# Keeping fourteen units of V and two heads' output weights on the chip between two attention layers

## The chip, the cores and the metric

The kernel runs on one core of one Trainium2 chip. The metric is the time of one execution in microseconds on the device. Before the change three runs took 177.41 to 177.56 us, with a median of 177.49 us.

## The reference, cut to what matters

Four tokens pass through attention, a gated layer, the same attention and the same gated layer again. Both attentions use the same weights and the same caches, and both gated layers the same three matrices, so everything that is read for the first half is needed again for the second half.

```
x = x + A(layernorm(x), k_cache, v_cache, wq, wo)
x = x + B(layernorm(x), w_gate, w_up, w_down)
x = x + A(layernorm(x), k_cache, v_cache, wq, wo)
x = x + B(layernorm(x), w_gate, w_up, w_down)

A: q = x @ wq               4 tokens, D = 512, 32 query heads of 128
   k, v = last 2048 rows of the caches, 8 heads shared by 4 query heads each
   softmax(q k / sqrt(128)) v, then @ wo
B: (sigmoid(x @ w_gate) * (x @ w_up)) @ w_down     inner size 1792
```

## The kernel before

**What is where.** Everything is counted in units of 256 columns of bf16 over 128 partitions, 64 KB. One head's K or V (four tokens' caches, 2048 rows each) is 32 units, 2 MB. `kt` holds the K of all eight heads (256 units) and stays for both attentions. `wo_sb` holds the output weights of all eight heads (64 units, 8 a head) and stays too. `arena` (75 units), `side` (31 units), `pb` and `pt` take turns with the rest. `pt` also holds the softmax weights of two heads at a time. `WHERE` (L426 to L442) says at which units each V and each weight matrix lies. V does not stay: attention 1 reads all of it into the arena, and attention 2 reads all of it again, the first two heads into `arena` and `side` and the other six into K blocks that attention 2 has done with.

**PSUM.** There are eight banks. In attention 1 banks 0 to 2 take the transposes of K (L728, copied out at L738), bank 3 the scores, 4 the turned softmax weights, 5 and 6 the products with V, and 7 sums the output projection. The first gated layer has its sums in banks 0, 1 and 2, and the second q projection (`project_q`, L678) in bank 5. In attention 2 banks 3 and 0 take the scores of even and odd heads, 1 and 2 the turned weights.

**The order of work.** `_Plan` records operations with the tokens they read and write. `_schedule` (L95) places them on the engines by estimated durations; `_assign_sync` (L185) gives each wait a semaphore. The DMAs alone stand in the order in which the program names them, all on SP's queue: SP waits until the destination of the next transfer is free, issues it (L456, in `dma`), and goes on. A transfer whose place is freed late holds back all behind it.

**Attention, head by head.** `scores` (L742) multiplies q with K (L751), takes the row maximum (L760 to L770), the exponential (ACT, L773), and turns the result (L779, L784). `weights` (L791) spreads it into `pt` (L806 on DVE, L813 on ACT). `pv_wo` (L863) multiplies with V, at L841 for heads marked in `WIDE` (followed by a copy at L849 and a sum at L856) and at L883 for the others, scales (L893), selects (L919, L926) and applies the output weights (L934). After head 6, `early_residual` (L941) takes the sum out of bank 7: a copy on ACT (L947), a subtraction on DVE (L953), eight matmuls on PE (L960) and an addition (L966). Head 7 goes a short way of its own (L904, L551, L554).

**Between the attentions** lies the first gated layer (`glu`, L1007): u01 and g01 (the first half of `w_up` and `w_gate`, which stay for the second gated layer), g23, u23, then `w_down` in pieces d0, d4, d8, d10, d12. g23 and d8 share arena units, so the transfer of d8 waits until the matmuls with g23 are over. Then the 32 units of `wq` that did not stay are read (q01), then V for attention 2.

**The end.** V of heads 6 and 7 arrives last, then g23, u23 and `w_down` for the second gated layer. Head 7's V comes in pieces of 16, 8 and 8 units.

```
WHERE["V0_%d" % (HKV - 1)] = [ar(0, 16), ar(16, 8), ar(24, 8)]
...
    "V2_0": [ar(22, 14), sx(0, 8), sx(8, 8), sx(16, 2)],
    "V2_1": [sx(18, NS - 18), ar(0, UHEAD - NS + 18)],
...
for h in range(2, HKV):
    WHERE["V2_%d" % h] = [("kt", (h - 2) * UHEAD + u, n)
                          for u, n in (((0, 16), (16, 8), (24, 8)) if h == HKV - 1 else ((0, UHEAD),))]
```

Of the kernel before, what the change touches and what calls it, by code (L numbers as in the profile page):

```python
# [6 lines left out]
BF16 = mybir.dt.bfloat16  # L7
ACTF = mybir.ActivationFunctionType
# [6 lines left out]
class _Op:  # L15
    __slots__ = ("idx", "eng", "name", "dur", "emit", "deps", "odeps", "users", "start", "finish",
                 "sem", "val", "inc", "dma_bytes", "dma_rate", "waits", "prio", "ndeps_left")

    def __init__(self, idx, eng, name, dur, emit):
        self.idx = idx  # L20
        self.eng = eng
        self.name = name
        self.dur = dur
        self.emit = emit
        self.deps = set()
        self.odeps = set()
        self.users = []
        self.start = 0.0
        self.finish = 0.0
        self.sem = None  # L30
        self.val = 0
        self.inc = 1
        self.dma_bytes = 0
        self.dma_rate = 0.0
        self.waits = ()
        self.prio = idx
        self.ndeps_left = 0
# [147 lines left out]
def _assign_sync(ops, order, n_dma_sems):  # L185
    counts = {}
    dma_i = 0
    for e in ENGINES:
        for o in order[e]:
            if o.sem is not None:  # L190
                sem = o.sem
            elif e == "sync":
                sem = ("dma", dma_i % n_dma_sems)
                dma_i += 1
                o.inc = 16
# [72 lines left out]
def build(nc, A_x, A_k, A_v, A_wq, A_wo, B_wg, B_wu, B_wd, out):  # L268
# [15 lines left out]
    NCH = 4  # L284
# [21 lines left out]
    WIDE = {0: {0: 4, 1: 4, 2: 4, 3: 4, 4: 4, 5: 4, 6: 2}, 2: {2: 2, 3: 2, 4: 2, 5: 2}}  # L306
    HEADS1 = list(range(HKV))
# [29 lines left out]
    with es:  # L337
# [24 lines left out]
        rz = sb("rz", [128, NPT * NR], F32)  # L362
# [40 lines left out]
        def blk_ap(s):  # L403
            return {"kt": kt, "ar": arena, "pt": pt, "pb": pb, "sx": side}[s[0]][:, s[1] * UNIT:(s[1] + s[2]) * UNIT]
# [15 lines left out]
        def ar(u, n):  # L420
            return ("ar", u, n)
# [5 lines left out]
        for h in range(HKV - 1):  # L427
            WHERE["V0_%d" % h] = [ar(MAIN - UHEAD if h % 2 == 0 else 0, UHEAD)]
        WHERE["V0_%d" % (HKV - 1)] = [ar(0, 16), ar(16, 8), ar(24, 8)]
        WHERE["u01"], WHERE["g01"] = ar(MAIN - 2 * GU, 2 * GU), ar(MAIN - 4 * GU, 2 * GU)  # L430
        WHERE.update({
            "g23_1": ar(32, 2 * GU), "u23_1": ar(0, 2 * GU),
            "d0_1": ar(14, 8), "d4_1": ar(22, 8), "d8_1": ar(32, 4), "d10_1": ("pb", 0, 4), "d12_1": ("pt", 4, 4),
            "q01": [ar(36, 10), ar(0, 14), ar(14, 8)],
            "V2_0": [ar(22, 14), sx(0, 8), sx(8, 8), sx(16, 2)],
            "V2_1": [sx(18, NS - 18), ar(0, UHEAD - NS + 18)],
            "g23_3": ar(22, 2 * GU), "u23_3": sx(0, 2 * GU),
            "d0_3": ar(0, 8), "d4_3": ar(8, 8), "d8_3": ar(38, 8), "d12_3": sx(14, 4),
        })
        for h in range(2, HKV):  # L440
            WHERE["V2_%d" % h] = [("kt", (h - 2) * UHEAD + u, n)
                                  for u, n in (((0, 16), (16, 8), (24, 8)) if h == HKV - 1 else ((0, UHEAD),))]  # L442
# [19 lines left out]

        def load_v(L, h):
# [3 lines left out]
            for s in WHERE["V%d_%d" % (L, h)]:  # L467
                n = s[2]
                dma("V%d_%d_%d" % (L, h, u0), blk_ap(s), v_d[h][:, :, u0 * UNIT:(u0 + n) * UNIT], w=blk_tok(s),
                    rate={32: "bw_16k", 16: "bw_8k"}.get(n, "bw_4k"), nbytes=128 * n * UNIT * 2)  # L470
# [207 lines left out]
        def project_q(L, pieces, pieces_last):  # L678
            if not L:
                return project_first(pieces, pieces_last)  # L680
            prev = []
            toks = []
            wid = NB
            for n, (ap, tk, ktc, q0, q1) in enumerate(pieces):
                def e_q(pe, ap=ap, ktc=ktc, q0=q0, q1=q1, st=(n == 0), last_ktc=pieces_last):
                    last = None
                    for q in range(q0, q1):
                        last = pe.matmul(ps[:, QB, q * wid:(q + 1) * wid],
                                         ap[:, (q - q0) * 128:(q - q0 + 1) * 128],
                                         xn[:, ktc * (NB + 1):ktc * (NB + 1) + wid],  # L690
                                         start=(st and q == q0), stop=(ktc == last_ktc),
                                         skip_group_check=True)
                    return last
                prev = [P.op("tensor", "qproj%d_%d" % (L, n), tm["pe_pair"] * (q1 - q0), e_q,
                             r=list(tk) + [("xn",)], w=[("psq", n)], banks=(QB,), order=prev)]
                toks.append(("psq", n))

            def scaled(src, r, banks):
                P.op("vector", "q_evac%d" % L, c_dve(HQ * NB),
                     lambda v: v.tensor_tensor(  # L700
                         qs[:, 28:28 + HKV * NB * STRIP].rearrange("p (h b s) -> p h b s", h=HKV, b=NB)[:, :, :, 0:REP],
                         src.rearrange("p (h r b) -> p h b r", h=HKV, r=REP)[:, :, 0:NB, :],
                         rstd[:, :].unsqueeze(1).unsqueeze(3).broadcast_to([128, HKV, NB, REP]),
                         ALU.mult),
                     r=r + [("rstd",)], w=[("qs",)], banks=banks)
            if True:
                mc = means(L, tq, cs_q, HQ)
                P.op("vector", "q_mean%d" % L, c_dve(HQ * NB),
                     lambda v: v.tensor_tensor(tq[:, :], ps[:, QB, 0:HQ * NB], tq[:, :], ALU.subtract),
                     r=toks + [mc], w=[mc], banks=(QB,))  # L710
                scaled(tq[:, :], [mc], ())
# [30 lines left out]
        def scores(L, n, h, sbk, tbk):  # L742
# [14 lines left out]
            P.op("tensor", "S%d_%d" % (L, h), 16 * tm["pe_s"] * (0.55 if L == 0 else 1.0), e_s, r=kr + [("qs",)], w=[("pss", sbk)], banks=(sbk,))  # L757
# [32 lines left out]

        def weights(L, n, h, tbk):  # L791

            k2 = n % 2
            kp = n % NPT
            ptv = pt[:, kp * NJ4 * NR:(kp + 1) * NJ4 * NR]
            pk = blk_tok(("pt", kp * NR // 4, NR // 4))
# [31 lines left out]
        def wide_pv(L, n, h, wide, bank, out, s):  # L828

            kp = n % NPT  # L830
# [4 lines left out]
            def e_pv(pe):  # L835
                last = None
                for i, (tv, q, c) in enumerate(steps):
                    w0 = (kp * NJ4 + (tv * NB + q) * NCH + c) * NR
# [3 lines left out]
                                     pt[:, w0:w0 + rows], v,  # L842
                                     start=(i < groups), stop=(i >= len(steps) - groups), skip_group_check=True)
                return last
            P.op("tensor", "PV%d_%d" % (L, h), 1800.0, e_pv,
                 r=blk_tok(s) + blk_tok(("pt", kp * NR // 4, NR // 4)) + (("pa", kp),), w=[("pvw", bank)], banks=(bank,))
# [16 lines left out]
        def pv_wo(L, n, h, pbk, pieces, prev=()):  # L863
            k2 = n % 2
            kp = n % NPT
            wide = WIDE[L].get(n, 0)
            obk = pbk[k2] if L else 6 if wide else 5
# [5 lines left out]
            for s, j0 in () if wide else pieces:  # L873
                def e_pv(pe, s=s, j0=j0):
                    last = None
                    for j in range(j0, j0 + s[2] * UNIT // 128):

                        q, c, tv = j // NJ, j % NJ // CB, j % CB
                        w0 = (kp * NJ4 + (tv * NB + q) * NCH + c) * NR
# [5 lines left out]
                                         pt[:, w0 - odd * NR:w0 + (2 - odd) * NR],  # L885
                                         start=(j == 0), stop=(j == NJ4 - 1), skip_group_check=True)
                    return last
                prev = [P.op("tensor", "PV%d_%d_%d" % (L, h, j0), s[2] * UNIT // 128 * tm["pe_pair"], e_pv,
                             r=blk_tok(s) + blk_tok(("pt", kp * NR // 4, NR // 4)) + (("pa", kp),), w=[("pso", obk, j0)], banks=(obk,), order=prev)]
# [79 lines left out]
        GB, UB, YB = 0, 1, 2  # L969

# [12 lines left out]
        def load_d(L, fc0, fc1):  # L983
# [3 lines left out]
            dma("wd%d_%d" % (L, fc0), blk_ap(s)[:, 0:(fc1 - fc0) * D], rows[:, (fc0 - g0) * D:(fc1 - g0) * D],  # L987
                w=blk_tok(s), rate="bw_4k")
# [18 lines left out]
        def glu(L, last_layer):  # L1007
            layer_norm(L)
# [68 lines left out]
            if not last_layer:  # L1077
                parts[-2:] = [(8, 10), (10, 12), (12, 14)]
# [56 lines left out]
        def load_wo(h):  # L1135
# [4 lines left out]
            else:  # L1140
                dma("wo_%d" % h, to, A_wo[h * REP * 128:(h + 1) * REP * 128, :].rearrange("(p j) n -> p (j n)", j=4),
                    w=[("wo", h)])
# [32 lines left out]

        glu(1, False)
# [14 lines left out]
        assert u0 == HQ  # L1191
        project_q(2, kept_q + streamed, 1)
# [101 lines left out]
```

## Time and profile before

| what | value |
|---|---|
| median of three runs | 177.49 us |
| the profiled execution's own time | 177.11 us |
| its span (first to last instruction) | 175.4 us |
| read from memory | 70.00 MB, 399 GB/s over the span |
| packets of the loads on SP's queue, share of 16 DMA engines' time | 96.1% |
| busy: PE, DVE, ACT | 78%, 55%, 41% |
| granted TensorE clock, mean | 0.825 |
| DMA issues on SP's queue | 62 |

The span is what the profile covers; the time of the same execution is 1.7 us more. The DMA row of the page gives, for each fortieth of the span, the mean busy share of the core's 16 DMA engines in tenths. The chain of waits is read backward from the last instruction: each step is what released the step after it. A duration before a name in the timeline is the time from the group's first start to its last end, and the square bracket at a line's end is how long the engine sat idle before it and what ended that. The trace also has every DMA packet with its start, its length in time and its size. 16 packets at a time are under way, each starting within about 4 ns of the end of the one before it on its engine, so that they can be strung together into 16 engines; the numbers of the engines are not in the trace.

### The profile page before, as it was taken

What the parts mean: (1) busy time and instruction counts of PE and PEld (TensorE: products, weight loads), DVE (VectorE), ACT (ScalarE), POOL (GpSimd) and SP (SyncE); (2) the same over time, 40 slices, a digit from 0 to 9 for tenths busy, and PEclk for the clock granted to TensorE, in tenths of its full rate; (3) what the DMA queues carried; (4) which work ended last, traced back from release to release, by engine and by line L of the source; (5) the groups of instructions that cost most, each with busy time, mean ns of one, the idle gap of its engine ahead of it and who ended that gap; (6) DMA issues with size and microseconds to landing.
All of it is one profiled execution on the core that took longest, in us unless ns stands there. A gap on an engine that the chain in (4) does not pass through costs nothing.

```text
span 175.4 us, 4862 instructions
## 1 busy us (share of the span) xinstructions
PE 137.2 (78%) x2175; PEld 101.4 (58%) x2175; DVE 97.1 (55%) x240; ACT 71.4 (41%) x125; POOL 6.8 (4%) x17
## 2 busy tenths in 40 slices
PE   0395699898998879988978877449769985978794
PEld 0392488656575657565654567438317753557693
DVE  7444015977848575795884432104298977372440
ACT  2064217848377728384472140300045644341400
POOL 5200000000000000000000002002000000000020
PEclk9999656999999978999999655555586999696858
DMA  5999999999999999999999999999999999999970
GB/s 192 419 424 419 432 441 419 426 419 428 422 419 437 404 441 434 417 426 404 441 422 390 403 420 417 396 403 421 402 427 435 424 426 422 434 405 414 416 285 14
DMA packets 9216, 70.31 MB, mean 401 GB/s; under 512 B 1000, under 2 KB 1772, under 8 KB 5996
## 3 DMA queue, kind: packets, MB, share of 16 engines
q1 hardware_dynamic: 9188, 70.00, 96.1%
q8 instruction: 17, 0.28, 0.6%
q14 instruction: 3, 0.02, 0.0%
q10 hardware_dynamic: 8, 0.00, 0.0%
HBM read 70.00 MB, written 0.00 MB: 399 GB/s over the span
## 4 chain that ended last, share of the span: by engine, by line
DMA 65%; PE 25%; DVE 5%; SPq 2%; ACT 1%; issue 1%; DVEq 0%; ACTq 0%
DMA arena<-in_A_v_cache_dram 31%; DMA kt<-in_A_k_cache_dram 12%; DMA kt<-in_A_v_cache_dram 11%; DMA arena<-in_B_w_down_dram 6%; PE ps L751 5%; DMA arena<-in_A_wq_dram 4%; PE ps L841 4%; PE ps L728 4%; PE ps L883 3%; PE ps L1023 2%; SPq L456 2%; PE ps L821 1%; PE ps L1092 1%; ACT pb L773 1%; DVE nmz L760 1%
## 5 line engine op out<-in xcount | busy, mean ns | idle before, releaser
L738 ACT COPY kt<-ps 128x1024 bf16<-128x1024 bf16 x40 | 39.1, 1017 | 28.0 <-PE ps L728 27.9
L728 PE MATMUL ps<-ident_r,kt 128*128 128x128 bf16 x512 | 40.2, 238 | 5.1 <-DMA kt<-in_A_k_cache_dram 3.2
L728 PEld LDWEIGHTS ps<-ident_r,kt 128*128 128x128 bf16 x512 | 34.7, 109 | 11.9 <-issue 4.4
L738 DVE COPY kt<-ps 128x1024 bf16<-128x1024 bf16 x24 | 29.2, 1215 | 14.1 <-PE ps L728 13.9
L751 PE MATMUL ps<-kt,qs 128*32 128x512 bf16 x256 | 19.2, 429 | 2.5 <-ACT pb L773 1.7
L773 ACT ACTIVATE pb<-ps,nmz 128x512 bf16<-128x512 f32 x16 | 11.1, 691 | 23.6 <-DVE nmz L770 22.1
L806 DVE TENSOR_TENSOR pt<-ps,ofbr 128x1024 bf16<-128x1024 f32 (+1 forms) x16 | 16.2, 1013 | 2.9 <-PE ps L784 2.9
L841 PE MATMUL ps<-arena,pt 128*64 128x512 bf16 (+1 forms) x128 | 13.2, 384 | 3.3 <-DMA arena<-in_A_v_cache_dram 3.3
L760 DVE TENSOR_REDUCE nmz<-ps 128x1 f32<-128x512 f32 x16 | 11.0, 686 | 6.7 <-PE ps L751 6.7
L779 DVE STREAM_TRANSPOSE pb<-pb 128x512 bf16<-128x512 bf16 x16 | 11.2, 700 | 5.1 <-ACT pb L773 5.1
L751 PEld LDWEIGHTS ps<-kt,qs 128*32 128x32 bf16 x256 | 6.0, 103 | 9.8 <-ACT pb L773 2.7
L813 ACT ACTIVATE pt<-ps,ofbr 128x96 bf16<-128x96 f32 x32 | 8.3, 343 | 8.0 <-PE ps L784 8.0
L841 PEld LDWEIGHTS ps<-arena,pt 128*64 128x64 bf16 (+1 forms) x128 | 6.0, 114 | 8.4 <-DMA arena<-in_A_v_cache_dram 4.3
L1023 PE MATMUL ps<-xn,arena 128*128 128x5 bf16 (+1 forms) x196 | 7.4, 172 | 2.6 <-DMA arena<-in_B_w_up_dram 1.1
L1023 PEld LDWEIGHTS ps<-xn,arena 128*128 128x128 bf16 x196 | 7.2, 117 | 2.9 <-DMA arena<-in_B_w_up_dram 1.2
L849 ACT COPY arena<-ps 128x512 f32<-128x512 f32 (+1 forms) x7 | 3.9, 556 | 12.1 <-PE ps L841 12.0
L621 POOL TENSOR_TENSOR rs<-pt,rs 128x4 f32<-128x4 f32 x4 | 4.1, 1014 | 119.7 <-DVE pt L617 119.7
L821 PE MATMUL ps<-rowf,nmz 128*128 128x16 f32 x32 | 7.4, 309 | 1.3 <-DVE pt L806 1.0
L821 PEld LDWEIGHTS ps<-rowf,nmz 128*128 128x128 f32 x32 | 6.0, 233 | 4.1 <-DVE pt L806 1.8
L856 PEld LDWEIGHTS ps<-arena 128*128 128x128 f32 x52 | 6.7, 201 | 2.1 <-ACT arena L849 1.6
L856 PE MATMUL ps<-arena 128*128 128x16 f32 x52 | 7.4, 273 | 0.7
L934 PE MATMUL ps<-wo_sb,onr 128*16 128x512 bf16 x56 | 6.0, 419 | 1.1 <-DVE onr L926 1.1
(127 smaller groups left out, 144.3 us busy)
## 6 DMA issues: line engine op xcount, KB each, us to landing
kt<-in_A_k_cache_dram SPq DMA_DIRECT2D x8, 2048.0 KB, 24.6
arena<-in_A_v_cache_dram SPq DMA_DIRECT2D x7, 2048.0 KB, 20.2
kt<-in_A_v_cache_dram SPq DMA_DIRECT2D x5, 2048.0 KB, 18.5
wo_sb<-in_A_wo_dram SPq DMA_DIRECT2D x8, 512.0 KB, 25.2
arena<-in_B_w_gate_dram SPq DMA_DIRECT2D x3, 896.0 KB, 9.7
arena<-in_B_w_down_dram SPq DMA_DIRECT2D x5, 512.0 KB, 21.6
kt<-in_A_wq_dram SPq DMA_DIRECT2D x1, 2048.0 KB, 11.7
side<-in_A_wq_dram SPq DMA_DIRECT2D x1, 1984.0 KB, 15.9
```

The source lines that it names most:

```text
L728: last = pe.transpose(bankb(bank)[:, (v * NB + q) * 128:(v * NB + q + 1) * 128], kt[:, c0:c0 + 128], ident_b[:, :])
L738: return (e.tensor_copy if ev == "vector" else e.copy)(to, fr)
L751: last = pe.matmul(ps[32 * b:32 * b + 32, sbk, 0:CB * 128], qs[:, q0:q0 + 32], blk_ap(kblk(h, b))[:, c * CB * 128:(c + 1) * CB * 128], sta ...
L760: lambda v: v.tensor_reduce(nmv, ps[:, sbk, 0:CB * 128], AXX, ALU.max, negate=True),
L773: o = a.activation(pbuf[:, :], ps[:, sbk, 0:CB * 128], ACTF.Exp, bias=gv, scale=1.0, accum_out=zv)
L779: P.op("vector", "ptr%d_%d" % (L, h), 650.0, lambda v: v.transpose(turned[:, :], pbuf[:, :]), r=[("pb", 0), ("pb", 1)], w=[("pb", 2), ("pb ...
L806: lambda v: v.tensor_tensor(pv4[:, 0:nj], spread(tbk, nj).unsqueeze(2).broadcast_to([128, nj, NB, REP]), ofb[:, :].unsqueeze(1).unsqueeze( ...
L813: last = a.mul(pv4[:, nj:NJ4, b, :], spread(MB, NJ4 - nj), ofb[:, b:b + 1])
L821: lambda pe: pe.matmul(ps[:, tbk, CB * NQ:CB * NQ + NR], zv.broadcast_to([128, 128]), rowf[:, :], start=True, stop=True),
L841: last = pe.matmul(ps[rows * g:rows * (g + 1), bank, 0:wide * 128].rearrange("p (c d) -> p c d", c=wide), pt[:, w0:w0 + rows], v, start=(i ...
L856: last = pe.matmul(ps[:, out[0], out[1]:out[1] + NR], part[:, c * 128:(c + 1) * 128], ey[wide][:, c * NR:(c + 1) * NR], start=(c == 0), st ...
L1023: last = pe.matmul(ps[:, bank, fc * wid:(fc + 1) * wid], cols[:, fc - g0, :], xn[:, ktc * (NB + 1):ktc * (NB + 1) + wid], start=(ktc == 0 ...
```

## The change

Three things are changed together.

**Output weights of heads 0 and 1 go to PSUM and back.** After the last K transpose, `stash(0)` copies the 16 units of `wo_sb` that hold these two heads to PSUM banks 3, 0, 1 and 2, four copies on DVE of 128x512 words. `stash(1)`, during the second q projection, copies them back, four copies on ACT. In between these 16 units of SBUF take g23, d9 and 14 of the 32 units of q01. The first gated layer's sums move to banks 5, 6 and 4, and the second q projection to banks 5 and 6: it is evacuated in two halves of 16 query heads, so that scores of heads 0 to 3 can start before the last piece of `wq`.

**Fourteen units of V stay in the arena** from attention 1: the last 8 units of head 6 (units 66 to 73) and the last 6 of head 7 (units 30 to 35). `load_v` does not read them in attention 2. u01 and g01 move down in the arena for that, `w_down` pieces d4 and d8 of the second gated layer go to freed K blocks, and head 7's softmax weights of attention 2 get a place of their own in a K block.

**Five units are read in another shape.** The last 3 units of head 2's output weights and the last 2 of d4 in the first gated layer are each read by two transfers, one over 124 rows and one over 4, instead of one over 128.

Some orders written out by hand for the end of attention 2 are dropped, and the estimated durations for the planner change.

```
-        WHERE["V0_%d" % (HKV - 1)] = [ar(0, 16), ar(16, 8), ar(24, 8)]
-        WHERE["u01"], WHERE["g01"] = ar(MAIN - 2 * GU, 2 * GU), ar(MAIN - 4 * GU, 2 * GU)
+        WHERE["V0_%d" % (HKV - 1)] = [ar(0, 16), ar(16, 10), ar(30, 6)]
+        WHERE["u01"], WHERE["g01"] = ar(52, 2 * GU), ar(38, 2 * GU)
+        PT3 = ("kt", 187, 4)
...
-            "g23_1": ar(32, 2 * GU), "u23_1": ar(0, 2 * GU),
-            "d0_1": ar(14, 8), "d4_1": ar(22, 8), "d8_1": ar(32, 4), "d10_1": ("pb", 0, 4), "d12_1": ("pt", 4, 4),
-            "q01": [ar(36, 10), ar(0, 14), ar(14, 8)],
-            "V2_0": [ar(22, 14), sx(0, 8), sx(8, 8), sx(16, 2)],
-            "V2_1": [sx(18, NS - 18), ar(0, UHEAD - NS + 18)],
-            "g23_3": ar(22, 2 * GU), "u23_3": sx(0, 2 * GU),
-            "d0_3": ar(0, 8), "d4_3": ar(8, 8), "d8_3": ar(38, 8), "d12_3": sx(14, 4),
+            "g23_1": ("ws", 0, 2 * GU), "u23_1": ar(0, 2 * GU),
+            "d0_1": ar(14, 8), "d4_1": ar(22, 8), "d8_1": ar(36, 2), "d9_1": ("ws", 14, 2), "d10_1": ("pb", 0, 4),
+            "d12_1": ("pt", 4, 4),
+            "q01": [("ws", 0, 8), ar(0, 14), ar(14, 4), ("ws", 8, 6)],
+            "V2_0": [ar(18, 12), ar(36, 2), sx(0, 16), sx(16, 2)],
+            "V2_1": [sx(18, NS - 18), ar(0, 18), ar(74, 1)],
+            "g23_3": ar(0, 2 * GU), "u23_3": sx(0, 2 * GU),
+            "d0_3": ar(14, 8), "d4_3": ("kt", 179, 8), "d8_3": ("kt", 192, 8), "d12_3": sx(14, 4),
...
+        WHERE["V2_6"] = [("kt", 128, 24), ar(66, 8)]
+        WHERE["V2_7"] = [("kt", 152, 16), ("kt", 168, 10), ar(30, 6)]
...
+        def dma_few(name, dst, src, cols, w, rate="bw_4k"):
+            n = dst.free_size() - cols
+            cut = [(0, 128, 0, n), (0, 124, n, n + cols), (124, 128, n, n + cols)]
+            def e_few(e):
+                return [e.dma_start(dst[a:b, c:d], src[a:b, c:d]) for a, b, c, d in cut]
...
+        STASH = ((0, 3), (4, 0), (8, 1), (12, 2))
+        def stash(back):
+            for u, b in STASH if back else STASH[1:] + STASH[:1]:
+                at = blk_ap(("ws", u, 4))
+                r, w = [("wo", u * UNIT // WOH)], [("st", b)]
+                if back:
+                    P.op("scalar", "back%d" % u, 1010.0, lambda a, b=b, at=at: a.copy(at, bankb(b)), r=w,
+                         w=r + list(blk_tok(("ws", u, 4))), banks=(b,))
+                else:
+                    P.op("vector", "stash%d" % u, 620.0,
+                         lambda v, b=b, at=at: v.tensor_scalar(ps[:, b, :].bitcast(I32), at.bitcast(I32), 0, None, ALU.bitwise_or),
+                         r=r, w=w + [("pst", b), ("pss", b)] + list(blk_tok(("ws", u, 4))), banks=(b,))
...
+            GB, UB, YB = (0, 1, 2) if last_layer else (QB, QB + 1, MB)
...
-                parts[-2:] = [(8, 10), (10, 12), (12, 14)]
+                parts[2:] = [(8, 9), (9, 10), (10, 12), (12, 14)]
```

## The prediction, made before the changed kernel was run

> **What bounds the kernel now.** I read the page's rows by slices and by queue first, then the chain of waits, then the timeline of three stretches.
>
> ```profile
> DMA  5999999999999999999999999999999999999970
> ...
> q1 hardware_dynamic: 9188, 70.00, 96.1%
> q8 instruction: 17, 0.28, 0.6%
> ```
>
> The DMA engines are busy from the second slice to the 38th: the kernel is one stream of 70 MB. Instruction packets (second queue) run on the same engines.
>
> ```profile
> 145.01 18.59 DMA kt<-in_A_v_cache_dram
> ...
> 163.65 0.58 PE ps L883 x16
> ...
> 164.25 0.21 DVE onb L893
> ...
> 164.51 0.57 PE ps L904 x16
> ```
>
> The chain waits for the last piece of head 7's V (landed 163.6). What follows it is one string of small steps to 175.4, so time saved ahead of 163.6 is saved at the end, if PE is ready for it.
>
> ```profile
> 158.58 1.87 PE L883 MATMUL ps<-pt,kt 128*128 128x32 bf16 x64 [0.90 <-DMA kt<-in_A_v_cache_dram]
> ...
> 161.09 1.03 PE L883 MATMUL ps<-pt,kt 128*128 128x32 bf16 x32
> ...
> 162.60 0.59 ACT L947 CAST pb<-ps 128x512 bf16<-128x512 f32 x1 [3.92 <-PE ps L934]
> ...
> 163.22 0.69 DVE L953 TENSOR_TENSOR pb<-ps,pb 128x512 bf16<-128x512 f32 x1 [1.93 <-ACT pb L947]
> 163.65 0.56 PE L883 MATMUL ps<-pt,kt 128*128 128x32 bf16 x16 [0.61 <-DMA kt<-in_A_v_cache_dram]
> 164.07 0.34 PE L960 MATMUL ps<-rqb,pb 128*128 128x4 bf16 x8
> ```
>
> Head 6's V lands (158.0) and starts a second string: 64 matmuls, selection, output weights, L947, L953, L960. It is nearly as late as head 7's.
>
> **The sixteen engines.** Strung together from the trace, data packets of 16 KB follow each other every 608 ns (26.9 bytes per ns and engine). The 17 instruction packets (also 16 KB) took 0.88 to 1.10 us, and each put its engine about 1.06 us behind. They fall on eight engines only, two each while the stream runs; the other eight get none. So a transfer lands in two groups: head 7's last piece lands on ten engines at 159.22 to 160.93 and on six at 162.05 to 163.05. PE waits for the last of the sixteen.
>
> **1. Fourteen units less.** A unit is 64 KB, 4 KB an engine: 4096/26.9 = 0.152 us, fourteen 2.13 us. Eight of them (1.22 us) stand ahead of head 6's landing, all ahead of head 7's.
>
> **2. Five units in another shape.** No row shows a transfer over 124 rows. Bounds: over all 16 engines nothing changes. Over fewer, those get more and the others less. The trace shows equal shares: 8 rows on each of 16 engines for 128 rows, and for the store at the end, of 4 rows, semaphore packets on four engines (980 such packets: 16 for each of 61 loads, and 4). Equal shares of 124 rows allow at most four engines, 31 rows each, and the 4 rows one more each. I take four. The other twelve are then free of five units, 5 x 0.152 = 0.76 us. The four get 32 packets of 1.5 KB and 32 of 1 KB; 1 KB packets follow every 43 ns, 2 KB every 80, so I put 1.5 KB at 62: 32 x (62 + 43) = 3.36 us, less the 0.76 they had, +2.6 us.
>
> The Trainium skill's "DMA: Bandwidth & Descriptors" (section "Why a DMA increments its semaphore by 16 and not by 1") says that a transfer runs on the largest number up to 16 that divides its rows, on the lowest-numbered engines; for 4 rows the trace agrees, for 124 no run here shows it yet, and by it the sum is the same.
>
> Which four, the trace doesn't say. If they are the earliest four (head 7's piece at 159.22 to 159.55), they land at up to 159.55 + 2.6 - 2.13 = 160.02, and the latest of the others at 163.05 - 0.76 - 2.13 = 160.16: level. If they are among the ten, the latest is at 161.4. If one is among the six, 163.5. I take the first: it needs the four to lie in the group without instruction packets, which a block of neighbours does if the group is a block too.
>
> **3. The end.** Head 6 (24 units): 158.02 - 0.76 - 1.22 = 156.04; +0.55, as in before, 156.6. In front, head 5's V lands at 153.13 - 0.76 = 152.4; from its first matmul to its output weights before took 3.5 us (153.64 to 157.16), so PE is free at 156.5. Then 48 matmuls, 64 having taken 1.87: 1.40, to 158.0. Scaling, selection, L926 as before (160.44 to 161.29): to 158.85. L934 now stands ahead of head 7's 32 matmuls, not behind: 0.5, to 159.4. L947 to 160.05, L953 to 160.8, L960 to 161.2. In the new order of PE the last 20 matmuls of head 7 stand behind L960: 16 took 0.56, so 0.70, to 161.9. Their data (160.16 + 0.57 = 160.7) has come. Before they ended at 164.21: **2.3 us earlier**. The landing gains 2.89, but L947 to L960 are late next. All after it is the same work.
>
> **4. The copies.**
>
> ```profile
> 93.27 0.26 DVE L825 RECIPROCAL rz<-ps 128x16 f32<-128x16 f32 x1 [1.67 <-PE ps L821]
> 94.27 0.69 DVE L760 TENSOR_REDUCE nmz<-ps 128x1 f32<-128x512 f32 x1 [0.74 <-PE ps L751]
> ...
> 99.33 1.23 DVE L806 TENSOR_TENSOR pt<-ps,ofbr 128x1024 bf16<-128x1024 f32 x1 [2.02 <-PE ps L784]
> ...
> 128.23 0.69 ACT L773 ACTIVATE pb<-ps,nmz 128x512 bf16<-128x512 f32 x1 [15.01 <-DVE nmz L770]
> ```
>
> To PSUM: no row has DVE copy SBUF to PSUM. Below, the fill of a bank (L530) took 0.485; above, the copy of 1024 elements (L738) 1.22. I take 0.69, L953's for 512. Two copies fit the idle 1.67 and 0.74 ahead of L825 and L760, the fourth the 2.02 ahead of L806. The third stands ahead of L926 (95.95) and makes it, and L934, 0.45 late; PE waits for V until 97.23 anyway. At 1.22 that would be 0.5 us past it, and u01's issue as much later. Cost 0; at worst 0.5.
>
> Back: ACT's copy of 1024 elements from PSUM took 1.017 (L738), four 4.1 us. ACT had been idle 15 us. The last two wait for the last piece of `wq`, and the first exponential is queued behind them; I put it at 127.0, against 128.23 before, since scores of head 0 now start before that piece. Cost 0; if that fails, 1 to 2 us of head 0's softmax, and V of head 0 is there only at 127.8.
>
> **5. SP's queue.** The stream must not run dry: from issue to the first packet of an idle queue was 1.45 us (first load), the smallest distance in the stream 1.62 (d8, issued 110.89, behind g23's matmuls). That wait goes; d8 to d12 can issue at about 105.5. The issues that move later: g01 from 99.39 to 100.5 (its place holds the matrix read by L856), distance 4.0 to 2.4; d0 by 1.1, 6.2 to 4.6; `side` (0,16) as one piece, 2.6 to about 1.8. g23 waits for the fourth copy (98.0) and goes behind g01. The second of V's blocks in `kt` waits for the scores of head 0, which come earlier. SP was held up to 4.1 us when about nine transfers were outstanding; the 31 packets on four engines may hold it so at 105, ahead of issues that have 5 us to spare. Cost 0.
>
> **The sum.** 177.11 (profiled execution; span 175.4) - 2.35 = 174.76. The median of runs is 0.38 above the profiled one: 177.49 - 2.35 = **175.1**.
>
> **Rivals.**
>
> No relief by the 124 rows, for either of two reasons: they are spread over all 16, or an engine's 26.9 bytes per ns is the rate at which its partitions take data, so that packets from four engines into everybody's partitions slow the others by what they save. Head 6 then lands at 156.8, all of step 3 is 0.76 later: gain 1.6, 175.9. For: all engines run at one rate. Against: an instruction packet, which goes to no such partition, delays its engine's data in full, as if the engine were the limit. The same page of the Trainium skill ("Where 436 GB/s comes from") calls the ports into SBUF the bottleneck, which speaks for this rival; no trace here separates the two.
>
> PE's clock. 32 matmuls of L841 took 1.90 us at 148.74, after an idle 1.0 us, and 1.06 at 153.64 with none. If head 5's run slowly, output weights end at 157.3 and step 3 starts 0.75 late: gain 1.6 again; with head 6's too, about 1.1, 176.4.
>
> Slower: one of the four engines is among the six late ones. Head 7 then lands at 163.05 + 2.6 - 2.13 = 163.5, its 20 matmuls end at 164.8 instead of 164.21: +0.6, 178.1. It decides from a landing of 162.95, where the four are 2.8 us behind the rest.
>
> **Chances.** Forecast 0.52; no relief 0.20; clock 0.12; the four late 0.16, of which 0.13 slower and 0.03 near nothing. 0.2% is 0.35 us, about what a measurement of this kernel can tell from no change. Faster 0.84, same 0.03, slower 0.13. The range is 174.4 (the full 2.89 with 0.2 to spare) to 176.5, which takes in the second and third case.
>
> **What would show it.** Right: 69.1 MB read; head 7's V 2.9 us earlier on the latest engine and the engines' spread at the end down from 3.8 us to below 3; L960 directly ahead of the last L883. Wrong: four engines last by more than 2 us; a slice of DMA below 9 between 100 and 130 us; L926 near 96 us waiting for a copy while V is there; the exponential of head 0 later than 128.2.

## The result, and the profile after

The change makes the kernel slower: 180.0 us median against 177.45 for the kernel before on the same chip, ratio 1.016, 95% interval 1.013 to 1.019. The ratios here and below leave out executions far slower than the rest of their kernel, and are not the quotients of the medians. The forecast was 175.1, range 174.4 to 176.5. The profiled execution took 179.37 us, its span 177.4.

The page of the changed kernel, rows by slices (40 slices of 4.4 us) and by queue:

```profile
DMA  4999999999999999999999999999999999999940
GB/s 178 447 418 407 431 425 440 429 414 419 436 336 388 418 431 425 415 437 414 429 424 397 394 408 419 401 342 406 366 377 448 412 425 440 415 412 419 410 191 6
...
q1 hardware_dynamic: 9748, 69.08, 95.3%
q8 instruction: 17, 0.28, 0.6%
```

0.92 MB less is read, as forecast, yet the DMA engines are as busy as before (95.3% against 96.1%): they need more time for fewer bytes. The DMA row shows nothing of it. The row below does: 336 and 388 GB/s at 49 to 58 us, 342, 366 and 377 at 115 to 133 us, where some 420 is usual. The first hole is where the split `wo_2` is read, the next where the split d4 is, the last two where V of head 0 is.

The timeline of the changed kernel at the end:

```profile
157.32 1.06 PE L863 MATMUL ps<-kt,pt 128*32 128x256 bf16 x32 [0.21 <-DMA kt<-in_A_v_cache_dram]
...
160.99 1.36 PE L906 MATMUL ps<-pt,kt 128*128 128x32 bf16 x48 [0.21 <-DMA kt<-in_A_v_cache_dram]
...
163.80 1.03 PE L906 MATMUL ps<-kt 128*128 128x32 bf16 x32
163.92 0.59 ACT L971 CAST pb<-ps 128x512 bf16<-128x512 f32 x1 [5.11 <-PE ps L958]
...
164.54 0.69 DVE L977 TENSOR_TENSOR pb<-ps,pb 128x512 bf16<-128x512 f32 x1 [1.33 <-ACT pb L971]
165.37 0.35 PE L984 MATMUL ps<-rqb,pb 128*128 128x4 bf16 x8 [0.54 <-DVE pb L977]
165.59 0.69 PE L906 MATMUL ps<-kt 128*128 128x32 bf16 x20
```

(L863, L906, L971, L977 and L984 were L841, L883, L947, L953 and L960.) V of head 6 starts its matmuls at 160.99, where 158.58 was the start before and 156.6 the forecast. From there to the end of the last 20 matmuls it takes 5.29 us; the forecast had 5.3. So the string behind the landing is as foreseen, and the landing is 4.4 us late.

The copies, in the timelines of DVE and ACT:

```profile
93.68 0.69 DVE L1005 TENSOR_SCALAR ps<-wo_sb 128x512 int32<-128x512 int32 x1
95.33 0.26 DVE L847 RECIPROCAL rz<-ps 128x16 f32<-128x16 f32 x1 [0.96 <-PE ps L843]
...
122.06 2.06 ACT L1001 COPY wo_sb<-ps 128x1024 bf16<-128x1024 bf16 x2 [6.79 <-DMA wo_sb<-in_A_wq_dram]
125.86 2.06 ACT L1001 COPY wo_sb<-ps 128x1024 bf16<-128x1024 bf16 x2 [1.75 <-DMA wo_sb<-in_A_wq_dram]
130.18 0.69 ACT L792 ACTIVATE pb<-ps,nmz 128x512 bf16<-128x512 f32 x1 [2.26 <-DVE nmz L789]
```

They cost what was assumed, 0.69 and 1.01 us each. The first exponential comes at 130.18, not 127.0, but behind a last piece of `wq` that is itself late.

**The sixteen engines, strung together from the packets.** Latest landing in us, of each transfer's sixteen engines (the runs e1 to e18 are described in the next section):

| kernel | V of head 2, attention 1 | first piece of `wq` | first piece of V of head 0 | V of head 6 | last streamed V of head 7 |
|---|---|---|---|---|---|
| before | 57.16 | 119.26 | - | 158.02 | 163.05 |
| changed | 59.31 | 121.55 | 127.21 | 160.44 | 164.48 |
| e1, all rows together | 57.18 | 119.25 | 124.95 | 158.20 | 162.25 |
| e11, e1 with the split `wo_2` | 59.28 | 120.18 | 125.89 | 158.00 | 162.05 |
| e9, e1 with V and TensorE's order changed | 57.26 | 119.13 | 124.95 | 156.91 | 160.97 |
| e17, e9 with the split `wo_2` | 59.39 | 120.22 | 126.59 | 158.72 | 162.79 |
| e16, e9 with both splits | 59.22 | 121.43 | 127.11 | 160.09 | 164.15 |

The second row loses 2.15 us at `wo_2` and never gets them back. The mechanism of step 2 is right: the 124 rows run on four engines with 31 packets each (16 semaphore packets more than e1: four engines for each of two pieces of two transfers), and those four have no instruction packets, as assumed. Their price is not. The four's 1.5 KB packets took 65 ns at first, then 109 on average between 51.3 and 54.2 us (62 assumed), and **while they ran, the other twelve engines' 16 KB packets took 782 ns (to 51.3 us) and 872 ns (after it) instead of the 616 of the same stretch in e9**. The twelve were to gain 0.46 us on these three units; they lost 0.8 (the fastest engine lands V of head 2 at 56.23 in e17, at 55.39 in e9).

### The profile page after: what moved, and what is told of

The parts are those of the page before. It is cut to its first block, busy times and chain, and to the rows that moved or that the text cites. A ratio compares the mean times of both kernels' runs of the same rounds, so it can differ in the third digit from the quotient of the medians.

```text
span 177.4 us, 4876 instructions
## 1 busy us (share of the span) xinstructions
PE 137.1 (77%) x2175; PEld 99.4 (56%) x2175; DVE 99.2 (56%) x246; ACT 75.5 (43%) x129; POOL 6.8 (4%) x17
## 3 DMA queue, kind: packets, MB, share of 16 engines
q1 hardware_dynamic: 9748, 69.08, 95.3%
## 4 chain that ended last, share of the span: by engine, by line
DMA 65%; PE 24%; DVE 4%; ACT 3%; SPq 1%; issue 1%; DVEq 0%; ACTq 0%
DMA arena<-in_A_v_cache_dram 31%; DMA kt<-in_A_k_cache_dram 12%; DMA kt<-in_A_v_cache_dram 12%; DMA wo_sb<-in_B_w_gate_dram 6%; PE ps L770 5%; DMA wo_sb<-in_A_wq_dram 5%; PE ps L863 5%; PE ps L747 4%; PE ps L1064 3%; PE ps L906 2%; SPq L463 1%; ACT wo_sb L1001 1%; PE ps L1133 1%; PE ps L710 1%; ACT pb L792 1%
## 5 line engine op out<-in xcount | busy, mean ns | idle before, releaser
L747 PE MATMUL ps<-ident_r,kt 128*128 128x128 bf16 x512 | 39.1, 233 | 4.1 <-DMA kt<-in_A_k_cache_dram 2.0
L747 PEld LDWEIGHTS ps<-ident_r,kt 128*128 128x128 bf16 x512 | 33.4, 106 | 11.2 <-issue 4.8
L770 PE MATMUL ps<-kt,qs 128*32 128x512 bf16 x256 | 20.5, 443 | 1.3 <-DVE qs L726 0.7
L863 PE MATMUL ps<-arena,pt 128*64 128x512 bf16 (+1 forms) x128 | 14.2, 386 | 4.9 <-DMA arena<-in_A_v_cache_dram 4.9
L828 DVE TENSOR_TENSOR pt<-ps,ofbr 128x1024 bf16<-128x1024 f32 (+1 forms) x15 | 15.4, 1030 | 2.9 <-PE ps L803 2.8
L863 PEld LDWEIGHTS ps<-arena,pt 128*64 128x64 bf16 (+1 forms) x128 | 6.2, 113 | 10.6 <-DMA arena<-in_A_v_cache_dram 5.9
L835 ACT ACTIVATE pt<-ps,ofbr 128x96 bf16<-128x96 f32 x28 | 7.2, 342 | 7.5 <-PE ps L803 7.5
L843 PE MATMUL ps<-rowf,nmz 128*128 128x16 f32 x32 | 6.6, 283 | 2.2 <-DVE pt L828 2.2
L958 PE MATMUL ps<-wo_sb,onr 128*16 128x512 bf16 x56 | 6.1, 411 | 2.6 <-DVE onr L950 2.6
L1064 PE MATMUL ps<-xn,arena 128*128 128x5 bf16 (+1 forms) x168 | 6.3, 172 | 2.0 <-DMA arena<-in_B_w_up_dram 1.1
L1001 ACT COPY wo_sb<-ps 128x1024 bf16<-128x1024 bf16 x4 | 4.0, 1012 | 8.6 <-DMA wo_sb<-in_A_wq_dram 8.5
L843 PEld LDWEIGHTS ps<-rowf,nmz 128*128 128x128 f32 x32 | 5.2, 204 | 4.3 <-DVE pt L828 3.1
```

The lines of the kernel that those rows point to most:

```text
L747: last = pe.transpose(bankb(bank)[:, (v * NB + q) * 128:(v * NB + q + 1) * 128], kt[:, c0:c0 + 128], ident_b[:, :])
L770: last = pe.matmul(ps[32 * b:32 * b + 32, sbk, 0:CB * 128], qs[:, q0:q0 + 32], blk_ap(kblk(h, b))[:, c * CB * 128:(c + 1) * CB * 128], sta ...
L828: lambda v: v.tensor_tensor(pv4[:, 0:nj], spread(tbk, nj).unsqueeze(2).broadcast_to([128, nj, NB, REP]), ofb[:, :].unsqueeze(1).unsqueeze( ...
L835: last = a.mul(pv4[:, nj:NJ4, b, :], spread(MB, NJ4 - nj), ofb[:, b:b + 1])
L843: lambda pe: pe.matmul(ps[:, tbk, CB * NQ:CB * NQ + NR], zv.broadcast_to([128, 128]), rowf[:, :], start=True, stop=True),
L863: last = pe.matmul(ps[rows * g:rows * (g + 1), bank, 0:wide * 128].rearrange("p (c d) -> p c d", c=wide), ptv[:, w0:w0 + rows], v, start=( ...
```

## The experiments

Medians in us, and ratios to the kernel before on the same chip. In the expectations, "the second experiment" is e1; "the sixth", "the ninth", "the eleventh", "the fifteenth" and "the sixteenth" are e6, e9, e11, e15 and e16. The letters of the theories are given anew in each group.

| run | us | ratio, 95% interval |
|---|---|---|
| e1_no_few | 178.09 | 1.0047, 1.0023 to 1.0072 |
| e2_only_few | 179.8 | 1.0166, 1.0137 to 1.0194 |
| e3_even_cut | 178.3 | 1.0092, 1.0056 to 1.0129 |
| e4_all_v | 178.65 | 1.0091, 1.0064 to 1.0118 |
| e5_cut_8_8_2 | 177.41 | 1.0009, 0.9983 to 1.0036 |
| e6_one_18 | 176.8 | 0.9977, 0.9952 to 1.0001 |
| e7_no_copy_back | 178.08 | 1.0061, 1.0040 to 1.0083 |
| e8_orders_kept | 177.96 | 1.0043, 1.0021 to 1.0065 |
| **e9_turns_late** | **175.98** | **0.9943, 0.9924 to 0.9961** |
| e10_before_18 | 177.25 | 1.0014, 0.9997 to 1.0031 |
| e11_few_wo_only | 178.03 | 1.0045, 1.0015 to 1.0074 |
| e12_eight_engines | 179.0 | 1.0111, 1.0083 to 1.0140 |
| e13_turns_all_v | 178.1 | 1.0053, 1.0034 to 1.0072 |
| e14_before_turns | 177.52 | 1.0011, 0.9986 to 1.0036 |
| e15_few_wd_only | 177.08 | 0.9985, 0.9952 to 1.0017 |
| e16_turns_few | 179.24 | 1.0119, 1.0086 to 1.0151 |
| e17_turns_wo | 177.25 | 1.0013, 0.9988 to 1.0037 |
| **e18_turns_wd** | **175.86** | **0.9932, 0.9914 to 0.9949** |

### Are the few engines the cause? (e1 to e4)

e1 takes the split away, e2 puts it alone on the kernel before, e3 cuts so that both parts run on sixteen engines, e4 is e1 without the fourteen units.

```
e1   FEW_WO, FEW_WD = {}, {}
e2   before.py + dma_few, FEW_WO, FEW_WD = {2: 3}, {(1, 4): 2}
e3   cut = [(0, 128, 0, n), (0, 112, n, n + cols), (112, 128, n, n + cols)]
e4   e1 + VKEEP = {}
```

> The changed kernel with all five units read over 128 rows again; everything else as changed. Theory F (the transfers over 124 and 4 rows run on four engines, slow the other twelve while they run and put the four behind, and all landings wait for the four): the whole loss goes and the fourteen units show, 175.5 to 176.3 us, 1.2 to 2 us under the kernel before. Theory T (the copies to PSUM and back, or the moved places between the attentions, cost the time): still 179 us or more. Theory I (three issues in place of one, SP held): 175.5 to 176.3 too, to be told from F by the run with 112 and 16 rows.

> The kernel before with one thing of the change: the same five units read over 124 and 4 rows. Nothing stays, nothing goes through PSUM. Theory F: slower than before by 3 to 4.5 us, 180.5 to 182 us. Theory T: within 0.5 us of before, or faster by up to 0.8 as the prediction had it. Theory I: as F.

> The changed kernel with the five units read over 112 and 16 rows in place of 124 and 4: as many transfers and issues, as small packets (1.5 and 1 KB), but 112 and 16 both divide by 16, so all sixteen engines share them, 7 rows and 1 row each. Theory F: like the run without few-row transfers, within 0.5 us. Theory I (issues, small packets): like the changed kernel, 179 to 181 us. Theory T: the same as the changed kernel.

> The changed kernel with the five units over 128 rows and all of V read again in attention 2, the fourteen units into the places where they would have stayed. Measures what the fourteen units are worth by themselves. By the prediction 2.13 us of stream, of which 1.6 show at the end: 1.3 to 2.2 us slower than the run without few-row transfers. Theory T would have it at 181 us.

The split alone makes the kernel before 1.7% slower, as much as the whole change does (1.6%), though by a little less than theory F had it. Windows of 2 us in the trace of e2 (DMA share and GB/s at the end of each line):

```profile
50.00:52.00 2.00, 2.00 (x31) 1.51 (x31) 1.37 (x4) 1.76 (x2) 0.00 (x0) 1.00 1.23 365
52.00:54.00 2.00, 1.49 (x26) 1.28 (x23) 2.00 (x3) 1.48 (x2) 0.00 (x0) 1.00 0.99 288
...
116.00:118.00 2.00, 0.56 (x16) 0.51 (x16) 0.41 (x3) 0.00 (x0) 0.00 (x0) 0.50 0.93 280
```

and of the kernel before in the same stretches:

```profile
50.00:52.00 2.00, 2.00 (x31) 1.50 (x32) 1.37 (x4) 1.70 (x2) 0.00 (x0) 1.00 1.06 438
52.00:54.00 2.00, 1.49 (x25) 1.28 (x23) 2.00 (x3) 1.53 (x2) 0.00 (x0) 1.00 1.06 453
...
116.00:118.00 2.00, 1.34 (x32) 1.09 (x32) 0.00 (x0) 0.00 (x0) 0.00 (x0) 0.50 1.06 409
```

The engines are busy all the time (share about 1) and move a sixth to a third less. But two things were left: e1 reads 0.92 MB less and is still 0.5% slower than before, and in e4 the fourteen units seem worth 0.44%, not 1.2%.

### Where e1 loses the rest: a stall of the stream (e5 to e7, e10)

e1's landings equal those of before up to V of head 0; then its stream stalls. Windows of e1 and of e11, whose fast engines come to the same transfers 2 us later:

```profile
124.00:126.00 2.00, 1.89 (x18) 0.51 (x19) 0.06 (x1) 1.59 (x2) 0.00 (x0) 0.50 1.02 317
126.00:128.00 2.00, 2.00 (x32) 0.79 (x28) 1.63 (x6) 0.10 (x1) 0.00 (x0) 0.56 0.72 253
128.00:130.00 2.00, 1.33 (x22) 0.45 (x18) 1.80 (x5) 0.71 (x3) 0.00 (x0) 1.00 0.93 379
```

```profile
124.00:126.00 2.00, 1.32 (x24) 0.68 (x25) 0.49 (x2) 1.47 (x2) 0.00 (x0) 0.50 1.01 403
126.00:128.00 2.00, 2.00 (x32) 0.69 (x24) 1.01 (x4) 0.56 (x1) 0.00 (x0) 0.50 1.01 416
128.00:130.00 2.00, 1.42 (x20) 0.39 (x16) 1.52 (x6) 0.78 (x2) 0.00 (x0) 0.80 1.05 434
```

Here, unlike above, the share itself falls (0.72): engines stand idle or held up in the 2-unit piece of V of head 0 and at the start of V of head 1, whose 6.5 KB packets took up to 1.83 us instead of 0.253. Both are issued by 122.05, and the fastest engine is there at 124.44.

```
e5   "V2_0": [ar(18, 12), ar(36, 2), sx(0, 8), sx(8, 8), sx(16, 2)]
e6   "V2_0": [ar(18, 12), ar(36, 2), sx(0, 18)]
e7   e1 without stash(1)
e10  before.py, "V2_0": [ar(22, 14), sx(0, 18)]
```

> The changed kernel without any transfer over 124 and 4 rows (as in the second experiment), and the 18 units of V of head 0 that go into the tile side cut 8, 8 and 2 as in the kernel before, not 16 and 2. In the second experiment's trace the stream moved only 216 to 300 GB/s between 124 and 129 us (420 around it), just as the 2-unit piece, 1 KB a packet, and the piece behind it ran. Theory C (the 16-unit piece ahead of the 2-unit piece makes the engines arrive there so that the small packets collide): the hole is gone, V of head 6 lands about 1.4 us sooner, and the time is about 177.0, some 1 us under the second experiment's. Theory B (ScalarE's copies back into wo_sb at 123.6 to 125.6 us make the hole) and theory D (any 1 KB piece at this place makes it): the hole stays and the time is within 0.3 us of 178.1.

> As the second experiment, but the 16 and the 2 units of V of head 0 in side are one transfer of 18 units, 9 KB a packet; no 1 KB packet of V is left there. Theory D (the 1 KB packets make the hole of 124 to 129 us) and theory C (their place behind a 16-unit piece): the hole is gone and the time is about 177.0. Theory B (the copies back): the hole stays, within 0.3 us of 178.1.

> As the second experiment, without ScalarE's four copies back from PSUM; the output weights of two heads of the second attention are then whatever lies in wo_sb, so a part of the computation is left out. Theory B: the stream shows no hole between 124 and 129 us and the time falls by 1 to 1.4 us to about 176.9. Theories C and D: the hole stays; the time falls by at most 0.3 us, to 177.8 or more, since the copies themselves cost the chain nothing after 130 us.

> The kernel before with one edit: the 18 units of V of head 0 in the tile side are one transfer of 9 KB packets, not 8, 8 and 2 units. If fewer packets there are worth something by themselves, it is 0.3 to 0.7 us faster than before; if the sixth experiment's gain only took away what the 16 and 2 cut had brought, it is within 0.2% of before, 177.0 to 177.4.

Theory B falls: without the copies back the hole is there (271 GB/s at 126 to 129 us) and the time is e1's, so step 4's price of zero for the copies back holds. Both other cuts of the piece help, by 0.4 and 0.7%, and e10 shows that the cut is worth nothing in the kernel before. But neither C nor D is clean: in e6, with no 1 KB packet of V in `side`, the 9 KB packets took up to 1.03 us and the stream moved 331 GB/s at 123 to 126 us. In e9 too, which has e6's cut, the stream moved 327 there. What these traces have in common is how soon after its issue the fastest engine reads the first piece of V in `side`: 1.4 to 2.0 us in e1, e6, e7, e9 and e15, where the slowest packets of that piece took 0.66 to 1.03 us, and 2.9 us in e11, where none took over 0.34. Why they wait was not settled, and this does not explain the 6.5 KB packets behind, which were issued 3.4 us ahead in e1 and as far ahead in e5, where none took over 0.46.

### TensorE's last string (e8, e9, e13, e14)

In the profiled executions of e5 and e6 V of head 5 is there at the same time (TensorE waits for it until 154.13 and 154.04), and the ends are 1.3 us apart (spans 174.3 and 175.6). The timeline of e5, then of e6:

```profile
154.13 1.06 PE L863 MATMUL ps<-kt,pt 128*32 128x256 bf16 x32 [0.18 <-DMA kt<-in_A_v_cache_dram]
...
157.18 0.39 PE L958 MATMUL ps<-wo_sb,onr 128*16 128x512 bf16 x4 [0.32 <-DVE onr L950]
157.85 1.42 PE L906 MATMUL ps<-pt,kt 128*128 128x32 bf16 x48 [0.27 <-DMA kt<-in_A_v_cache_dram]
```

```profile
154.04 1.90 PE L863 MATMUL ps<-kt,pt 128*32 128x256 bf16 x32 [0.18 <-DMA kt<-in_A_v_cache_dram]
...
158.56 0.60 PE L958 MATMUL ps<-wo_sb,onr 128*16 128x512 bf16 x4 [0.32 <-DVE onr L950]
159.09 1.46 PE L906 MATMUL ps<-pt,kt 128*128 128x32 bf16 x48
```

Between 155 and 160 us the granted clock is 0.84 on average in e5 and 0.50 in e6. In e5 TensorE still waits for head 6's V, in e6 that V waits for TensorE. Head 6's matmuls start 1.24 us later at the lower clock; this is one execution of each. e8 puts the hand-written orders of before back; e9 writes others for the new pieces, so that no matmul that only feeds head 5 or 6 stands ahead of V that has come:

```
e9 = e6 +   ops["WO2_5"].odeps.update(six)          # behind head 6's 48 matmuls
            seven[1].odeps.add(ops["sel2_6"])
            ops["WO2_6"].odeps.add(seven[1])         # behind head 7's 32
            ops["w_turn2"].odeps.add(seven[2])       # behind head 7's last 20
e13 = e9 +  VKEEP = {}
e14 = before.py with these in place of its own last orders; only head 5's output weights move
```

> As the second experiment, with the orders that the kernel before wrote out by hand for the last heads of the second attention put back (output weights of a head ahead of the next head's V, turns behind the sums). In the second experiment the 48 matmuls of head 6's V began at 160.15 us though its V had landed at 158.20, behind head 5's 32 matmuls at half the clock and its output weights. Theory O (the dropped orders cost that time): TensorE is free for head 6 by about 159 us and the time falls by 0.5 to 1 us, to about 177.3. Theory K (the granted clock is what makes them late; the order only moves the same work): within 0.3 us of 178.1.

> As the sixth experiment (no transfer over 124 rows, 18 units of V of head 0 in one transfer), with TensorE's last string in another order: head 6's 48 matmuls ahead of head 5's output weights, head 7's first streamed 32 ahead of head 6's output weights, its last 20 ahead of the turned sums. In the sixth experiment's trace TensorE ran that string at a granted clock of 0.50 and stood still in it for 0.29, 0.32, 0.29, 0.32 and 0.54 us behind VectorE, and the 16 matmuls of L928 began at 164.77. Theory T (the end is TensorE's string, not the stream): most of these 1.8 us go, L928 begins near 163.8, and the time falls by 0.7 to 1.1 us, to about 175.9. Theory S (the stream sets the end): within 0.3 us of 176.8.

> The ninth experiment, but all 64 units of V of heads 6 and 7 are read for the second attention; no unit stays. 0.92 MB more are read, 2.13 us of stream at 0.152 us a unit and engine. If the stream now sets the end (theory S): 175.98 + 2.1 = 178.1, or 177.7 if 1.7 us of it show. If TensorE's string still hides most of it, as in the fourth experiment: 0.4 to 0.8 us, 176.4 to 176.8.

> The kernel before, with the ninth experiment's order written for its last string: only the four matmuls of head 5's output weights move, behind head 6's 64 matmuls. In the trace of before TensorE waits 0.90 us for V of head 6 and 0.61 us for the last piece of V of head 7, so the stream sets its end. Theory: within 0.2% of before, 176.8 to 177.4; if the order by itself is worth what it gave the ninth experiment, 0.8 us less, 176.2.

The timeline of e9:

```profile
153.73 1.06 PE L863 MATMUL ps<-kt,pt 128*32 128x256 bf16 x32 [0.17 <-DMA kt<-in_A_v_cache_dram]
...
157.42 1.39 PE L906 MATMUL ps<-pt,kt 128*128 128x32 bf16 x48 [0.95 <-DMA kt<-in_A_v_cache_dram]
158.74 0.60 PE L958 MATMUL ps<-wo_sb,onr 128*16 128x512 bf16 x4
...
159.91 1.04 PE L906 MATMUL ps<-kt 128*128 128x32 bf16 x32 [0.33 <-DMA kt<-in_A_v_cache_dram]
160.88 0.60 PE L958 MATMUL ps<-wo_sb,onr 128*16 128x512 bf16 x4
161.48 0.72 PE L906 MATMUL ps<-kt 128*128 128x32 bf16 x20
162.99 0.35 PE L984 MATMUL ps<-rqb,pb 128*128 128x4 bf16 x8 [0.80 <-DVE onb L917]
```

TensorE now waits for V of head 6 and for the first piece of head 7's, not V for TensorE, and the six runs lie between 175.82 and 176.13; e6's lay between 175.69 and 177.45. **e9 is faster than both kernels**, and theory T of its expectation holds. The old orders (e8) do not help, and in the kernel before the new one is worth nothing (e14), since its string already waited for V. e13 against e9: the fourteen units are worth 2.12 us by the medians; step 1 said 2.13. A part of it is e13's own: the order holds head 6's output weights behind a piece of V that lands later there (TensorE waits for it until 162.87). The landings say it without this: the last streamed V lands 2.08 us earlier in e9 than in the kernel before. But only 1.05 us of it show in e9's time against that kernel. In the chain of waits of e9, the last piece of V no longer stands at the end:

```profile
160.95 0.57 PE ps L958 x3
...
161.54 0.59 ACT pb L971
...
162.16 0.69 DVE pb L977
...
162.99 0.35 PE ps L984 x8
```

From the first streamed piece of head 7's V, whose matmuls begin at 159.91, it goes through head 6's output weights (L958) to L971, L977 and L984, the steps that the prediction named as late next (L947 to L960 then).

### What a split transfer costs (e11, e12, e15 to e18)

```
e11  changed, FEW_WD = {}          e15  changed, FEW_WO = {}
e12  changed, 120 and 8 rows
e16  e9 + both splits    e17  e9 + wo_2's    e18  e9 + d4's
```

> The changed kernel with only wo_2 over 124 and 4 rows; the two units of layer 1's down weights go over all 128. The pair of them cost 1.9 us (180.0 against 178.1 in the second experiment). If the price goes by the bytes that four engines carry, three units of five: about 179.2. If only what is late near the end counts (the down weights, 115 us): about 178.3. If the issue at 51 us carries it all, since every later landing then waits for the four engines: about 180.

> The changed kernel with only the two units of layer 1's down weights over 124 and 4 rows; wo_2 goes over all 128. The eleventh experiment (only wo_2) ran at 178.03, the second (neither) at 178.1, the changed kernel (both) at 180.0. If the two units at 115 us carry the price: about 180. If it needs both, because the four engines' lag of the first is still there when the second comes: 178 to 178.7.

> The changed kernel with the same five units cut over 120 and 8 rows, so that the rows divide by eight and not by four only. Theory F (the packets of few engines slow all the others and make every landing wait for those few): with eight engines the lag is half as long, and the time is about 179.0. Theory N (more issues and more semaphore packets cost it): as the changed kernel, about 180.

> The ninth experiment with both transfers over 124 and 4 rows put back. If the few engines' price is the stream's (every landing waits for four engines that carry 31 packets more), it shows in full: 175.98 + 1.9 = about 177.9. If it was the string's at the lower clock, started later: 176.0 to 176.6.

> The ninth experiment with only wo_2 over 124 and 4 rows. Theory A (four engines are late by a fixed amount, and only what exceeds the lag of the engines that were last anyway shows): the eleventh's landings were 1.1 us behind the ninth's (V of head 6 at 158.00 against 156.91), so about 177.0, and half of the sixteenth's price. Theory Z (one such transfer is free, two are not): 175.8 to 176.2.

> The ninth experiment with only the two units of down weights over 124 and 4 rows. Theory A: the four engines' lag at 117 us is some 1.7 us, of which about 0.5 to 1.1 shows: 176.5 to 177.1. Theory Z: 175.8 to 176.2. If the relief of the other twelve pays here, as the fifteenth experiment's 177.08 against 178.1 could be read: 175.0 to 175.7.

On e1, either split alone seemed free: e11's V of head 6 lands 0.2 us before e1's, because its later engines do not run into the stall. e11 alone would fit "only what is late near the end counts"; e15, the late one alone, refutes that. That e15 ran 1.0 us faster than e1 was not followed up. On e9 the account is plainer: `wo_2`'s split costs 1.27 us, d4's nothing (175.86, not to be told from 175.98), both 3.26, more than e16's expectation had. Theory A had e17 right and e18 wrong (176.5 to 177.1), theory Z the other way round. What fits all three is theory A with the slack counted, an account made after the runs. At `wo_2` (51 us) the latest engines lie 1.87 us behind the fastest; the four, three at the front and one 1.08 behind, are set back by some 2.05 us against the fastest, which is itself 0.8 slower. So they become the last, and V of head 2 lands 2.1 us later. At d4 (115 us) instruction packets have put the latest engine of e9 3.2 us behind, and there is room for one split, if the first has not used it up. With both, the four come to lie up to 3.9 us behind the fastest.

e12 is not what its expectation says. Its semaphore packets (1058 against 1012 without a split) say 15 and 8 engines for 120 and 8 rows, not eight: 46 = 2 x (15 + 8); e3's 1076 say 16 and 16. By the Trainium skill's "DMA: Bandwidth & Descriptors" (section "Why a DMA increments its semaphore by 16 and not by 1"), the largest number up to 16 that divides the rows: the traces agree, 124 on 4, 120 on 15, 112 on 16. So e12 and e3 show that any split costs something here (0.6 and 0.4% over e1; 1.5 KB packets took 80 and 76 ns on average, a third more per byte than the 616 ns of 16 KB), and four engines about as much again. The interval of e3 overlaps that of e1, so its 0.4% is not certain.

The slowing of the others is not a matter of few engines, though. While the 1.5 KB packets ran, the 16 KB packets that started before 51.3 us took 867 ns on average in e3, where all sixteen engines share the split (731 for those that started later), and 1021 in e12 (775). Nor is it the small size alone: in the kernel before, 1 KB packets of a load over 128 rows ran on five to ten engines at 95.0 to 95.7 us, and the 16 KB packets that started beside them took 612 ns. What the loads over 124, 120 and 112 rows have in common is that an engine's share is not the eight rows that it has of 128. Whether that is the cause was not tried.

## Why the prediction was wrong, by its steps

**1. Fourteen units less: right in size, hidden at first.** 2.13 forecast; 2.08 by the last landing of V (the kernel before against e9), 2.12 by the time of e13 against e9. In e1 against e4 it showed as 0.44%, with TensorE's string and the stall in the way, and in e9 against the kernel before as 1.05 us.

**2. Five units in another shape: this step failed.** Where the sum counted 0.76 us gained, both splits cost 3.26 us on e9 (e16), and alone on the kernel before 1.7% (e2). The number of engines and which group they are in were right. Three assumptions were not. The other twelve gain nothing while the four work, they lose: 782 to 872 ns for 16 KB where 616 is usual. The four's packets took 109 ns on average once the first were through, not 62. And the early engines' lead was set against the sum of both transfers at the end, when the first one already makes the four last at 59 us, and every wait on a landing passes that on: TensorE later, so SP's issues later (u01 at 100.42, 99.01 before), so the fastest engines held up there: first packets of u01 of up to 0.91 us, 0.29 at most before. Of the 4.4 us by which head 6 is late, 0.76 is the relief that did not come, 3.2 what both splits cost e9, and some 0.4 is left, with the stall in it. The rival "no relief" had a cause of this kind, packets into everybody's partitions that slow the other engines; it assumed they slow them by what they save. They slow them by more. The Trainium skill's "DMA: Bandwidth & Descriptors" (section "Where 436 GB/s comes from"), with the ports into SBUF as the bottleneck, fits; that it is the ports and not another shared part was not tried.

**3. The end: right behind the landing, wrong in what makes TensorE ready.** 5.29 us from head 6 to the last 20 matmuls, against 5.3. "PE is free at 156.5" took head 5's string at 3.5 us. It is 3.44 in e5 (154.13 to 157.57) and 5.1 at the granted clock of 0.50 (154.04 to 159.16 in e6): the rival "PE's clock", which priced it at 0.84 us (1.90 against 1.06 for 32 matmuls) where the whole string took 1.7 longer. In the profiled execution of the changed kernel the string ran at the full clock (157.32 to 160.78), so there the clock is not why it is slow. In e1, at 0.50 from 155 to 160 us, it is a part of it: head 6's V landed at 158.20 and its matmuls began at 160.08.

**4. The copies: right.** 0.69 and 1.01 us each, and no time gained without the copies back (e7 against e1). The copies to PSUM were not taken away by themselves; with them, e1 issues u01 at 99.15 (99.01 before) and its landings keep up with those of before.

**5. SP's queue: the price of zero was wrong.** It named the place, "`side` (0,16) as one piece, 2.6 to about 1.8": in e1 that piece is issued at 120.22 and first read at 121.93, 1.7 later, and there the stall begins. It costs e1 at least some 1.3 us of head 6's landing (158.20; 156.91 in e9, cut otherwise, which has a smaller stall of its own).

**The rivals.** With the splits gone and the cut and the order mended, head 6 lands at 156.91 in e9, where "no relief" said 156.8. That e9's 175.98 is close to its 175.9 is luck: the rival said 1.6 us less than the kernel before, and e9 is 1.05 below that kernel on its own chip (177.03). The slower case (178.1) had another mechanism, and its end was 1.9 us short: the four were among the early ones, and it happened all the same.

## What to carry to other kernels

Where every landing waits for the last of sixteen engines, ask of a transfer not how many bytes it moves but how late it makes its slowest engine, at that point of the stream and not at the end; and look at GB/s, not at the busy share, which stayed at 9. Before pricing a saving in the stream, check whether TensorE would be ready at the lower of its clocks: an order that lets it wait for data, not data for it, was worth 0.6 to 0.8 us here (e9 against e6, by the ratios and by the medians), and nothing in the kernel before (e14). Two costs that meet at the same spot (a stall and a lag) do not add, so undo them on a base without the other.

## What the runs showed of the hardware

- A load over 124 rows uses four engines, and while it runs the others' 16 KB packets take 782 to 872 ns, not 616. With loads over 112 and 16 rows, on all sixteen, it was 867 at first; beside 1 KB packets of a load over 128 rows it was 612.
- 120 rows run on 15 engines and 8 rows on eight.
- Packets of a transfer that the fastest engine reached 1.4 to 2.0 us after its issue took up to 0.66 to 1.03 us (e1, e6, e7, e9, e15); reached 2.9 us after it, none of them took over 0.34 (e11). In e1 the transfer behind stalled too, up to 1.83 us for 6.5 KB (0.253 usual). The cause stays open.
- Of two executions that reach head 5's V at the same time (e5, e6), one had TensorE at 0.50 of its clock between 155 and 160 us, the other at 0.84: 32 matmuls took 1.90 and 1.06 us.
